# A gated mix of attention and FFN for one token: w_down's load moves from SyncE's queue to ScalarE's

## The chip, the cores and the metric

The kernel runs on one core of a Trainium2 chip. The metric is the device time of one execution in microseconds, the median of several runs. A core has TensorE (PE in the profile), VectorE (DVE), ScalarE (ACT), GpSimd (POOL) and SyncE (SP), and 16 DMA engines that bring data from the chip's main memory (HBM) into its own memory. In this kernel SyncE only issues DMAs.

## The reference

Four requests, one token each, float32. `x` is (4, 1, 512), there are 32 heads of 128, and 4096 cached positions for each head.

```python
q = (x @ wq).reshape(B, Sq, H, Dh).transpose(0, 2, 1, 3)
scores = einsum("bhqd,bhkd->bhqk", q, k_cache) * Dh ** -0.5
o = einsum("bhqk,bhkd->bhqd", softmax(scores), v_cache)
a = o.transpose(0, 2, 1, 3).reshape(B, Sq, H * Dh) @ wo        # wo: 4096 x 512
b = (gelu(x @ w_gate) * (x @ w_up)) @ w_down                   # w_down: 1792 x 512
g = sigmoid((x * gate_w).sum(-1, keepdims=True))
out = g * a + (1 - g) * b
```

The two caches are 537 MB of the 565 MB that are read.

## The kernel before, in words

The heads are taken in 8 groups of 4, and each group for each of the 4 requests: 32 blocks (`NT`). A block has 8 MB of keys and 8 MB of values, each with 64 KB on each of the 128 partitions. For a block VectorE multiplies the keys with the query (L379) and sums the products (L385), ScalarE takes the exponentials (L397), and TensorE multiplies them with the values (`pv`, L411).

All large data lie in one buffer, `big`. The keys alternate between two overlapping places at its front. The values of every block but the last lie at `VA`, and those of the last block at 0, in the place of old keys. What comes last reuses the same places: wo's first half lies in the first half of the values' place (`W0 = VA`), w_down in its second half (`D0 = VA + TW // 2`), and wo's second half in the place of the last keys (`W1 = TW`).

A small recorder, `Plan`, takes steps in the order in which the code is written. Each step names its engine and what it reads and writes in `big` or in a tile, and from that come the semaphore waits. Each engine plays its own steps in order. A DMA is a step of the engine that issues it, and the lane named with it gives the semaphore that its landing raises. `load` (L255) records every DMA as a step of SyncE, so all loads stand in one queue, in order. A step that waits holds up what stands behind it on its engine.

After the last block's scores come, in this order on SyncE's queue: the last values (lane `vl`), w_down (3584 KB), wo's first half (4096 KB in one DMA), and wo's second half in seven pieces, the last of them 128 KB each. w_down and wo's first half wait for `pv` of the last block but one, which frees the place at `VA`; wo's second half waits for the last scores.

On TensorE the tail runs as follows. `pv(NT - 1)` multiplies the last values. `turn_o(0)` transposes the attended rows of the first 16 heads (L455), `gather` collects the last group (L428), VectorE weighs it (L441), and `turn_o(1)` transposes the second 16 heads. ScalarE copies what `pv` left (`gather_a`, L419) and spreads the transposed rows (L471). Then 41 products are summed in the tile `wide` (`project_wide`, L485, which the page also shows with `hT`): 14 with the rows of w_down (`ffn_down`), 16 with the rows of wo's first half, 11 with rows of the second half. Since all of them are on TensorE, they run in the order of the code, whatever has landed. `fold` copies `wide` (L499) and adds up its four strips (L493), the last five rows of wo are multiplied in strips of their own (also L493), the result is copied (L600, L602) and stored (L603).

Of the kernel before, what the change touches and what calls it, by code (L numbers as in the profile page):

```python
# [19 lines left out]
class Plan:  # L20
# [18 lines left out]
    def add(self, engine, emit, reads=(), writes=(), lane=None, unit=1):  # L39
        lane = lane or engine  # L40
        self.units[lane] = unit
        row = self.by_lane.setdefault(lane, [])
        step = Step(lane, engine, emit, self.turn if engine in self.loops else None)
        step.at = len(row)
        need = {}
        for accesses, writing in ((reads, False), (writes, True)):
            for name, lo, hi in accesses:
                for other, a, b, wrote in self.past.get(name, ()):
                    if a < hi and lo < b and (wrote or writing):
                        if other.lane == engine and engine == "pe":  # L50
                            continue
                        if other.lane == engine and not wrote:
                            continue
                        need[other.lane] = max(need.get(other.lane, -1), other.at)
        seen = self.seen[engine]
        for l, n in sorted(need.items(), key=lambda x: -len(self.by_lane[x[0]])):
            if seen.get(l, -1) >= n:
                continue
            other = self.by_lane[l][n]
            other.asked = True  # L60
            step.waits[l] = n
            seen[l] = n
            for k, v in self.knew[other].items():
                seen[k] = max(seen.get(k, -1), v)
        step.waits = {l: n for l, n in step.waits.items()
                      if not any(self.knew[self.by_lane[m][k]].get(l, -1) >= n for m, k in step.waits.items() if m != l)}
        self.knew[step] = dict(seen)
        self.knew[step][lane] = step.at
        if row and lane == engine:
            for k, v in self.knew[row[-1]].items():  # L70
                if k != lane:
                    self.knew[step][k] = max(self.knew[step].get(k, -1), v)
        for accesses, writing in ((reads, False), (writes, True)):
            for name, lo, hi in accesses:
                old = self.past.get(name, [])
                if writing:
                    old = [x for x in old if not (lo <= x[1] and x[2] <= hi)]
                self.past[name] = old + [(step, lo, hi, writing)]
        row.append(step)
        self.steps.append(step)  # L80
        return step
# [51 lines left out]
def tile_gated_mix(tc: tile.TileContext, x, kc, vc, wq, wo, w_gate, w_up, w_down, gate_w, out):  # L133
    nc = tc.nc
    P = 128
    B, H, S, D = kc.shape
    DM = x.shape[2]
# [7 lines left out]
    NT = B * NG  # L145
    TW = R * D
# [4 lines left out]
    FC = F // P  # L151
# [62 lines left out]
    Q0, F0, F1, W0, D0 = VA, VA, VA + KC * F, VA, VA + TW // 2  # L214
# [4 lines left out]
    def place(a, n):  # L219
        return big[:, a:a + n]  # L220

    def z(a, n):
        return ("big", a, a + n)
# [15 lines left out]
    add = plan.add  # L239
# [14 lines left out]
    def load(dst, src, writes, lane):  # L254
        return add("sp", lambda: nc.sync.dma_start(dst, src), (), writes, lane=lane, unit=16)  # L255
# [10 lines left out]
    def VAT(i):  # L266
        return VA if i < NT - 1 else 0
# [3 lines left out]
             [z((F0, F1)[s], KC * F)], f"f{s}")  # L271

    def load_d():
        load(place(D0, FC * DM), w_down.rearrange("(p i) n -> p (i n)", i=FC), [z(D0, FC * DM)], "k")

    def load_w(w):
        src = wo[w * HW * D:(w + 1) * HW * D].rearrange("(p e) n -> p (e n)", e=E)
# [156 lines left out]
    def weigh(g):  # L434
        dve(lambda: V.reciprocal(ri, sm[:B * HT, D:]), t("sm"), t("ri"))
        s = sm[:B * HT, :D].rearrange("q (k e) -> q e k", e=E)
        if g < NG - 1:
            dve(lambda: V.tensor_scalar(ON[:, bass.ds(row(g), 1)], s[:, None], ri, None, op0=OP.mult), t("sm", "ri"),
                [("on", g * D, g * D + D)])
        else:  # L440
            dve(lambda: V.tensor_scalar(OX[:, :, GW - 1], s[:, :, None].to_broadcast([B * HT, E, HT, D // E]), ri, None,  # L441
                                        op0=OP.mult), t("sm", "ri"), [z(OXA, OXN)])
# [9 lines left out]
    def turn_o(w):  # L452
        def emit():
            for e in range(E):
                last = T.transpose(oT[:, e], OX[:, e].rearrange("q g h k -> q (g h k)"), ident[:B * HT, :B * HT])  # L455
            return last

        pe(emit, [z(OXA, OXN)] + t("ident"), t("oT"))
# [7 lines left out]
    def spread(w):  # L466
        n = (E, WIDE)[w]
        a, m = ES + w * E * 32, E - n
        dst = place(a, n * 32).rearrange("p (e k) -> p e k", k=8)
        src = T1[w][:, :n * B, None].to_broadcast([P, n * B, 8])  # L470
        act(lambda: A.activation(dst, src, AF.Copy), t(f"t1{w}"), [z(a, n * 32)])  # L471
        if m:
            a += n * 32
            dst2 = place(a, m * 32).rearrange("p (e k b) -> p e k b", k=8, b=B)
            src2 = T1[w].rearrange("p (e b) -> p e b", b=B)[:, n:, None, :].to_broadcast([P, m, 8, B])
            act(lambda: A.activation(dst2, src2, AF.Copy), t(f"t1{w}"), [z(a, m * 32)])
# [5 lines left out]
    def project_wide(s, w, reads):  # L482
        n = next(wide_rest)
        c = n % 4
        pe(lambda: T.matmul(wide[32 * c:32 * c + 32, :], s, w, start=n < 4, stop=n >= NW - 4), reads, t("wide"))  # L485
# [41 lines left out]
    def ffn_down(f0, f1):  # L527
        for f in range(f0, f1):
            a = D0 + f * DM
            project_wide(hT[:, f, :], place(a, DM), [("hT", f * 32, f * 32 + 32), z(a, DM)])  # L530
# [5 lines left out]
    for i in range(NT):  # L536
# [29 lines left out]
        if i > 0 and b == 0:  # L566
            weigh(g - 1)
    plan.turn = None
    load_d()
    load_w(0)  # L570
    load_w(1)
# [6 lines left out]
    gather(NG - 1)  # L578
    expand(1)
    weigh(NG - 1)  # L580
    ffn_down(0, 2)
    turn_o(1)
    turned(1)
    spread(1)
    ffn_down(2, FC)
    for e in range(E):
        project_wide(*attended(0, e))
    for e in range(WIDE):
# [56 lines left out]
```

## Time and profile before

| What | Value |
| --- | --- |
| median of 3 runs | 1309.47 us (1309.22 to 1309.71) |
| span of the profiled execution | 1308.2 us |
| mean granted TensorE clock | 0.637 |
| VectorE busy | 1155.2 us, 88% |
| TensorE busy | 355.4 us, 27% |
| ScalarE busy | 87.4 us, 7% |
| read from HBM | 564.67 MB, 432 GB/s over the span |

The span runs from the first to the last instruction of one profiled execution. No time is recorded for that execution beside its span; the median of the runs is 1.3 us more. All times in the views count from the span's start. In a view of instructions a row has the start, the duration, the engine, the line and operation, the tile written and the tiles read, the count, and in brackets how long the engine had been idle before and what ended that. "SPq" is SyncE issuing DMAs; "PEld" is TensorE loading weights, which overlaps its products. Matmuls are pipelined, and their ends are modelled.

### The profile page before, as it was taken

The numbers are of one execution on the slowest core, as the hardware profiler recorded it, in microseconds if no ns is written. First come the engines' busy times: TensorE is split into PE (matmuls) and PEld (weight loads), VectorE is DVE, ScalarE is ACT, GpSimd is POOL, SyncE is SP. The second block draws the span as 40 slices with busy tenths as digits, with TensorE's granted clock in tenths as the row PEclk, the third lists the DMA queues.
The fourth block names the chain that finished last, engine by engine and source line by source line (L and its number), as shares of the span: only waits on it lengthen the run. The fifth ranks groups of instructions, "written<-read, shape, count | busy, mean of one in ns | idle before, by whom it ended". The sixth has DMA issues, their size and how long they took to land.

```text
span 1308.2 us, 6148 instructions
## 1 busy us (share of the span) xinstructions
PE 355.4 (27%) x2504; PEld 100.7 (8%) x2504; DVE 1155.2 (88%) x299; ACT 87.4 (7%) x291; POOL 0.7 (0%) x6
## 2 busy tenths in 40 slices
PE   2402233212332211322321223331133222122327
PEld 0100001000010000100000000100001000010003
DVE  1899999999899998989989898998989899898991
ACT  0000000000000000000000000000000000000001
POOL 0000000000000000000000000000000000000000
PEclk9656666556676656666655666655566665666668
DMA  9999999999999999999999999999999999999998
GB/s 417 419 445 421 445 419 445 429 437 439 431 439 427 439 427 443 423 445 429 437 437 431 439 429 439 427 441 425 443 425 443 435 433 439 429 439 427 439 428 369
DMA packets 10977, 564.81 MB, mean 432 GB/s; under 512 B 1228, under 2 KB 1484, under 8 KB 1880
## 3 DMA queue, kind: packets, MB, share of 16 engines
q1 hardware_dynamic: 10968, 564.69, 99.7%
q8 instruction: 6, 0.10, 0.0%
q14 instruction: 3, 0.02, 0.0%
HBM read 564.67 MB, written 0.01 MB: 432 GB/s over the span
## 4 chain that ended last, share of the span: by engine, by line
DMA 72%; DVE 26%; PE 1%; issue 1%; SPq 0%; ACT 0%; DVEq 0%; POOLq 0%
DMA big<-in_A_k_cache 66%; DVE sc L385 13%; DVE big L379 12%; DMA big<-in_A_wo 2%; DMA big<-in_B_w_up 2%; DMA big<-in_A_x 2%; PE po L325 1%; PE q L506 0%; PE acc L493 0%; SPq L255 0%; PE wide L485 0%; DVE hT L525 0%; DVE m L390 0%; DVE xT L312 0%; DVE big L523 0%
## 5 line engine op out<-in xcount | busy, mean ns | idle before, releaser
L379 DVE TENSOR_TENSOR big<-big,qb 128x4096 f32<-128x4096 f32 x64 | 555.9, 8687 | 87.8 <-DMA big<-in_A_k_cache 87.8
L385 DVE TENSOR_REDUCE sc<-big 128x32 f32<-128x4096 f32 x64 | 555.9, 8686 | 2.3
L411 PE MATMUL po<-big,PM 128*32 128x512 f32 x2048 | 296.0, 743 | 899.9 <-DMA big<-in_A_v_cache 899.9
L411 PEld LDWEIGHTS po<-big,PM 128*32 128x32 f32 x2048 | 72.8, 133 | 1116.9 <-DMA big<-in_A_v_cache 824.7
L397 ACT ACTIVATE PM<-sc,nb 32x128 f32<-32x128 f32 x128 | 67.2, 525 | 478.0 <-DVE nb L392 431.3
L419 ACT ACTIVATE o<-po 128x512 f32<-128x512 f32 x16 | 9.6, 597 | 448.5 <-PE po L411 448.5
L397 ACT ACTIVATION_READ_ACCUMULATOR PM<-sc,nb 32x1 f32 x128 | 26.1, 204 | 0.0
L369 ACT ACTIVATE qb<-q 128x512 f32<-128x512 f32 x8 | 4.8, 597 | 246.9 <-PE q L367 246.9
L428 PE MATMUL sm<-o,sel 128*16 128x128 f32 x128 | 15.4, 273 | 5.1 <-ACT o L419 5.1
L312 DVE COPY xT<-sg 128x128 f32<-128x128 f32 x4 | 0.9, 282 | 17.9 <-PE sg L307 17.9
L506 PE MATMUL q<-big,xT 128*32 128x448 f32 x64 | 10.9, 853 | 15.4 <-DMA big<-in_B_w_gate 11.3
L461 DVE TENSOR_TENSOR tm<-oT,gmask 128x256 f32<-128x256 f32 x2 | 0.8, 425 | 13.8 <-PE oT L455 13.8
L428 PEld LDWEIGHTS sm<-o,sel 128*16 128x16 f32 x128 | 11.7, 97 | 12.8 <-ACT o L419 11.4
L602 DVE COPY res<-acc 4x128 f32<-4x128 f32 x1 | 0.3, 278 | 11.9 <-PE acc L493 11.9
L367 PE MATMUL q<-QM,hc 128*128 128x512 f32 x16 | 9.5, 678 | 4.2 <-DVE hc L363 4.2
L390 DVE TENSOR_REDUCE m<-sc 128x1 f32<-128x128 f32 x32 | 9.2, 286 | 1.1
L325 PE MATMUL po<-big,xT 128*32 128x512 f32 x64 | 8.5, 693 | 1.0 <-DVE xT L312 1.0
L391 DVE STREAM_TRANSPOSE mt<-m 128x32 f32<-128x32 f32 x32 | 6.8, 211 | 1.1
L485 PE MATMUL wide<-big 128*32 128x512 f32 x54 | 6.6, 597 | 1.2 <-DMA big<-in_A_wo 1.2
L392 DVE TENSOR_REDUCE nb<-mt 128x1 f32<-128x32 f32 x32 | 6.0, 186 | 1.1
L307 PE MATMUL sg<-ident,big 4*128 4x4 f32 x4 | 0.6, 254 | 23.2 <-DMA big<-in_A_x 23.2
L342 DVE TENSOR_TENSOR big<-po,amask 128x512 f32<-128x512 f32 x2 | 1.3, 686 | 5.8 <-PE po L325 5.8
(72 smaller groups left out, 58.6 us busy)
## 6 DMA issues: line engine op xcount, KB each, us to landing
big<-in_A_wo SPq DMA_DIRECT2D x1, 4096.0 KB, 27.5
big<-in_B_w_gate SPq DMA_DIRECT2D x1, 3584.0 KB, 17.4
big<-in_B_w_up SPq DMA_DIRECT2D x1, 3584.0 KB, 26.4
big<-in_B_w_down SPq DMA_DIRECT2D x1, 3584.0 KB, 18.2
big<-in_A_wo SPq DMA_DIRECT2D x2, 1024.0 KB, 25.4
big<-in_A_wo SPq DMA_DIRECT2D x2, 768.0 KB, 29.1
big<-in_A_k_cache SPq DMA_DIRECT2D x32, 29.7
big<-in_A_v_cache SPq DMA_DIRECT2D x32, 29.3
```

The lines of the kernel that those rows point to most:

```text
L325: last = T.matmul(PO[s][32 * j:32 * j + 32].rearrange("p j d -> p (j d)"), xTf[:, c, :32], w[:, n0:n0 + HB * D], start=c == 0, stop=c == K ...
L367: pe(lambda: T.matmul(q.rearrange("p b d -> p (b d)"), HC.rearrange("p h k -> p (h k)"), QM.rearrange("p b d -> p (b d)"), start=True, sto ...
L379: dve(lambda: V.tensor_tensor(k, k, QB[:, b:b + 1, :].to_broadcast([P, r1 - r0, D]), op=OP.mult), m + t("qb"), m)
L385: dve(lambda: V.tensor_reduce(SC[i % 2][:, r0:r1], k, axis=AX.X, op=OP.add), [z(KA(i) + r0 * D, (r1 - r0) * D)], [(f"sc{i % 2}", r0, r1)])
L390: dve(lambda: V.tensor_reduce(M1[n], SC[n], axis=AX.X, op=OP.max), t(f"sc{n}"), t(f"m1{n}"))
L391: dve(lambda: V.transpose(MT, M1[n].to_broadcast([P, PH])), t(f"m1{n}"), t("mt"))
L397: last = A.activation(PM[:, PZ:].rearrange("p (c m) -> p c m", m=32)[s, :, h:RJ * HT:HT], SC[n][s, :].rearrange("p (c j) -> p c j", j=RJ), ...
L411: last = T.matmul(PO[n][32 * c:32 * c + 32].rearrange("p j d -> p (j d)"), PM[:, m0:m0 + 32], place(VAT(i) + j * N, N), start=b == 0 and j ...
L419: act(lambda: A.activation(O[n], PO[n], AF.Copy), t(f"po{n}"), t(f"o{n}"))
L428: T.matmul(sm[:B * HT, :D], selv[:, j, m0:m0 + B * HT], O[n][:, j, :], start=(n, j) == (0, 0), stop=(n, j) == (N - 1, RJ - 1))
L485: pe(lambda: T.matmul(wide[32 * c:32 * c + 32, :], s, w, start=n < 4, stop=n >= NW - 4), reads, t("wide"))
L506: last = T.matmul(q.rearrange("p b d -> p (b d)")[32 * j:32 * j + 32, :FG], xTf[:, c, :32], place((F0, F1)[s] + c * F + j * FG, FG), start ...
```

## The change

w_down's load becomes a step of ScalarE: ScalarE's own queue issues it, under a lane of its own (`d`). The step names the place of the last values as read, so ScalarE waits until they have landed and then issues. The products with w_down's rows, of which two stood ahead of `turn_o(1)` and twelve behind `spread(1)`, all stand behind `spread(1)`.

```diff
     def load_d():
-        load(place(D0, FC * DM), w_down.rearrange("(p i) n -> p (i n)", i=FC), [z(D0, FC * DM)], "k")
+        add("act", lambda: nc.scalar.dma_start(place(D0, FC * DM), w_down.rearrange("(p i) n -> p (i n)", i=FC)),
+            [z(VAT(NT - 1), TW)], [z(D0, FC * DM)], lane="d", unit=16)
...
     weigh(NG - 1)
-    ffn_down(0, 2)
     turn_o(1)
     turned(1)
     spread(1)
-    ffn_down(2, FC)
+    ffn_down(0, FC)
```

On SyncE, at the end of its queue, the difference of the two programs is one row; the names are the source of each DMA, the shapes are partitions by elements:

```order
 L255 DMA big<-in_A_k_cache 128x16384
 L255 DMA big<-in_A_v_cache 128x16384 x2
-L255 DMA big<-in_B_w_down 128x7168
 L255 DMA big<-in_A_wo 128x8192
 L255 DMA big<-in_A_wo 128x2048 x2
```

wo's first half now stands right behind the last two blocks' values.

On ScalarE the changed program has this, from the last block's exponentials (`PM`) to the spread rows; its lines are one higher than before, and the brackets name the lane that a step waits for:

```order
L398 ACTIVATE PM,RS<-sc,nb 32x32x4 [waits lane_pe,lane_dve]
L398 ACTIVATE PM,RS<-sc,nb 32x32x4 x3
L274 DMA big<-in_B_w_down 128x7168 [waits lane_vl]
L420 ACTIVATE o<-po 128x512 [waits lane_pe]
L472 ACTIVATE big<-t 128x512 [waits lane_dve]
```

The DMA is new there, ahead of the copy of what `pv` left; the other rows are those of before.

On TensorE, the tail of the program before, from the last blocks' products with the values to the last wide product:

```order
L411 MATMUL po<-big,PM 32x512 x128
L455 MATMUL oT<-ident,big 128x16 x16
L428 MATMUL sm<-o,sel 16x128 x8
L430 MATMUL sm<-ones,RS 16x1
L485 MATMUL wide<-big,hT 32x512 x2
L455 MATMUL oT<-ident,big 128x16 x16
L485 MATMUL wide<-big,hT 32x512 x12
L485 MATMUL wide<-big 32x512 x27
```

And the same stretch now:

```order
L412 MATMUL po<-big,PM 32x512 x128
L456 MATMUL oT<-ident,big 128x16 x16
L429 MATMUL sm<-o,sel 16x128 x8
L431 MATMUL sm<-ones,RS 16x1
L456 MATMUL oT<-ident,big 128x16 x16
L486 MATMUL wide<-big,hT 32x512 x14
L486 MATMUL wide<-big 32x512 x27
```

All 14 products with w_down's rows (those that read `hT`) stand in one run behind the second transposes, and wo's 27 wide products follow them as before.

## The prediction

> **What bounds the kernel now.** I read the page first: shares of the span, DMA queues, the chain that ended last, DMA issues.
>
> ```profile
> span 1308.2 us, 6148 instructions
> q1 hardware_dynamic: 10968, 564.69, 99.7%
> HBM read 564.67 MB, written 0.01 MB: 432 GB/s over the span
> DMA 72%; DVE 26%; PE 1%; issue 1%; SPq 0%; ACT 0%; DVEq 0%; POOLq 0%
> big<-in_A_wo SPq DMA_DIRECT2D x1, 4096.0 KB, 27.5
> big<-in_B_w_down SPq DMA_DIRECT2D x1, 3584.0 KB, 18.2
> ```
>
> One queue, SP's, moves everything, and its packets fill the 16 DMA engines for 99.7% of the span. The kernel is a stream of 565 MB at 432 GB/s, 27 GB/s for each engine. The change leaves the bytes alone, so it acts only through the order in which the last ones arrive, and through what TensorE still has to do after them. So the second view is the timeline of the tail (columns: start, us, engine, line, operation, tiles, count, and in brackets the idle time before it and what ended that).
>
> ```profile
> 1268.09 0.33 SPq L255 DMA_DIRECT2D big<-in_B_w_down  x1
> 1268.46 10.66 SPq L255 DMA_DIRECT2D big<-in_A_wo  x8
> 1276.81 0.20 ACT L397 ACTIVATION_READ_ACCUMULATOR PM<-sc,nb 32x1 f32 x1
> 1277.99 9.95 PE L411 MATMUL po<-big,PM 128*32 128x512 f32 x64 [9.96 <-DMA big<-in_A_v_cache]
> 1288.01 0.60 ACT L419 ACTIVATE o<-po 128x512 f32<-128x512 f32 x1 [10.99 <-PE po L411]
> 1288.96 1.92 PE L428 MATMUL sm<-o,sel 128*16 128x128 f32 x16
> 1290.77 1.02 PE L485 MATMUL wide<-big,hT 128*32 128x512 f32 x3
> 1292.07 1.17 PE L455 MATMUL oT<-ident,big 16*128 16x16 f32 x16 [0.27 <-DVE big L441]
> 1293.17 2.78 PE L485 MATMUL wide<-big,hT 128*32 128x512 f32 x24
> 1296.12 4.50 PE L485 MATMUL wide<-big 128*32 128x512 f32 x40 [0.17 <-DMA big<-in_A_wo]
> 1302.76 1.06 PE L485 MATMUL wide<-big 128*32 128x512 f32 x6 [0.79 <-DMA big<-in_A_wo]
> 1303.87 0.60 ACT L499 ACTIVATE big<-wide 128x512 f32<-128x512 f32 x1 [8.96 <-PE wide L485]
> 1305.93 0.14 PEld L493 LDWEIGHTS po<-big 128*32 128x32 f32 x4 [0.17 <-DMA big<-in_A_wo]
> 1306.77 0.29 SPq L603 DMA_DIRECT2D out<-res  x1
> ```
>
> The last values land at 1278.0, where TensorE stops waiting for them. w_down lands at 1268.09 + 18.2 = 1286.3, wo's first half at 1268.46 + 27.5 = 1296.0, and the last bytes of wo about 1305.9. TensorE has nothing to catch up: w_down's rows are multiplied before wo's first half is there, so at 1296.12 and at 1302.76 it is TensorE that waits for data. The wide products end at 1302.76 + 1.06 = 1303.82, and 2.95 us later (the copy, the fold, the last five rows) the result is issued; only 0.17 us of that is a wait for wo. The tail is tight: whatever delays the wide products delays the end.
>
> **The change part by part.** *SP's queue.* It loses one issue (0.33 us). wo's first half takes w_down's place behind the last values, released by the same event (the product before the last), so the engines have no gap. wo's second half still waits for the last scores. Cost 0.
>
> *ScalarE's queue.* The new wait stands behind the last exponentials, which end at 1276.81 + 0.20 = 1277.0, and ahead of the copy of the last values' product, which ran at 1288.01 because TensorE let it. So ScalarE waits 1 us for the landing at 1278.0, issues, and has 10 us to spare. Cost 0 on the engine; without that cover every us of waiting would delay the copy by as much.
>
> *When w_down lands.* No row shows two large streams at once, so I bound it. The transfer starts at 1278.0 plus the time from an issue to its first bytes; the result's DMA needs 1308.2 - 1306.77 = 1.4 us for issue, transfer and landing together, so I take 1.0: 1279.0. Earliest: ScalarE's queue is served alone, 3.67 MB at 432 GB/s = 8.5 us, 1287.5. Latest: it is served after all of wo, about 1305.9. Between: SP has 8.4 MB of wo to move from 1277.5, so it stays busy, and equal shares give w_down 216 GB/s: 17.0 us, 1296.0, and 1296.3 with some tenths for the landing. I take the equal share, since the only foreign packets in this trace (instruction fetches, below) are let in among SP's packets and neither push them all aside nor wait for the end. wo's last bytes stay at 1305.9, since the sum of bytes is the same.
>
> *TensorE.* The two products that stood ahead of the second set of transposes saved nothing there: the transposes waited 0.27 us for VectorE anyway. Now they, the other 12, and the 27 wide products of wo, 41 in all, stand behind w_down's landing. The price of one is read off the weight loads, four for two products (each product is two records, so x40 is 20):
>
> ```profile
> 1278.82 0.22 PEld L411 LDWEIGHTS po<-big,PM 128*32 128x32 f32 x4 [0.63 <-issue]
> 1279.67 0.23 PEld L411 LDWEIGHTS po<-big,PM 128*32 128x32 f32 x4 [0.63 <-issue]
> ...
> 1297.40 0.16 PEld L485 LDWEIGHTS wide<-big 128*32 128x32 f32 x4 [0.27 <-issue]
> 1297.83 0.16 PEld L485 LDWEIGHTS wide<-big 128*32 128x32 f32 x4 [0.27 <-issue]
> ```
>
> 0.43 us for two at full clock, 0.215 each; 0.85 us, 0.425 each, at half. At full clock: 41 x 0.215 = 8.8, and 4.50 - 20 x 0.215 = 0.2 until the last is out. 1296.3 + 8.8 + 0.2 = 1305.3 instead of 1303.82 is 1.5 late; the 0.17 us wait at the end goes, since wo is there by then: **+1.3 us**. wo's wide rows are there by 1302.7, before their turn.
>
> *The clock.* TensorE now has nothing to do from 1292.07 + 1.17 = 1293.2 to 1296.3, 3.1 us, and little before. Windows of the trace (start:end and length, busy time of the engines, granted clock, DMA share, GB/s):
>
> ```profile
> 1190.00:1195.10 5.10, 0.04 (x4) 0.00 (x0) 5.10 (x1) 0.00 (x0) 0.00 (x0) 1.00 0.95 411
> 1195.10:1197.00 1.90, 0.00 (x0) 0.00 (x0) 1.83 (x3) 0.00 (x0) 0.00 (x0) 0.50 1.11 483
> 1258.60:1263.40 4.80, 4.77 (x24) 1.36 (x28) 4.77 (x2) 0.00 (x0) 0.00 (x0) 0.50 1.01 437
> 1263.40:1268.00 4.60, 4.60 (x44) 1.22 (x36) 4.60 (x1) 0.00 (x0) 0.00 (x0) 1.00 1.05 456
> 1268.00:1270.20 2.20, 0.03 (x4) 0.00 (x0) 2.20 (x1) 0.00 (x0) 0.00 (x0) 1.00 1.07 454
> 1270.20:1278.00 7.80, 0.01 (x2) 0.04 (x3) 6.08 (x8) 2.11 (x8) 0.00 (x0) 0.50 0.90 391
> 1278.00:1283.80 5.80, 5.80 (x28) 1.53 (x32) 0.00 (x0) 0.00 (x0) 0.00 (x0) 0.50 1.02 440
> ```
>
> The clock fell to half 2.2 us after the product that ended at 1268.0, and 5.1 us after the one that ended at 1190.0; once work began again it stayed at half for 4.8 us (from 1258.6) and 5.8 us (from 1278.0). Work at half clock loses half its time: 2.4 to 2.9 us, or nothing if the clock holds. An idle of 3.1 us is past the first of these falls by 0.9 and short of the second by 2.0; if the small transposes weigh little, the pause counts from the end of the gathering products (1288.96 + 1.92 = 1290.9), 5.4 us, and is past both. I take a fall, and the shorter recovery: **+2.4 us**. The Trainium skill, page "TensorE: Matmul & The Clock Gate", section "HAM oscillation — how this bites in real kernels", puts the limit at idle gaps of about 3.4 us. By that alone 3.1 us would be short enough and the sum would stay at +1.3; the 2.2 us row shows a fall earlier than that.
>
> Sum: +1.3 + 2.4 = **+3.7 us**. The span 1308.2 becomes 1311.9; the median of the runs before lies 1.3 above the span, so 1309.47 + 3.7 = **1313.2**.
>
> **The rivals.** *Equal shares, but the clock holds:* +1.3, **1310.8**. For it: the fall after 5.1 us. Against: the fall after 2.2.
>
> *Changing queues costs time.* The one place where another queue gets packets in the middle of the stream (3 us, 16 engines, so 48 us of engine time):
>
> ```profile
> q1 hardware_dynamic: 19, 1.25, 96.7%
> q8 instruction: 1, 0.02, 2.0%
> ```
>
> One 16 KB instruction packet held its engine for 2.0% of 48 = 0.96 us, where 27 GB/s makes 0.61: 0.35 more. w_down has 128 partition rows, 8 for each engine; 8 x 0.35 = 2.8 us on w_down's landing (1299.1) and on the end of the stream. With the half clock: +3.7 + 2.8 = +6.5, **1316.0**; without, 1313.6. Against: that packet went to an instruction buffer, not to big.
>
> *w_down last*, at 1305.9: the 41 products start there, 9.6 later than forecast, +13.3, **1322.8**. Nothing in the trace speaks for a preference for SP.
>
> *Served ahead, or at SP's pace in one piece:* w_down by about 1287.5, wo's first half by 1296.0 as before: **1309.5**, no change.
>
> *Faster.* Two queues keep the engines fuller. From 1277.5 to 1305.6 the 12.06 MB of w_down and wo's two halves ran at 429 GB/s; at the 454 of the window after 1268.0 they need 26.6 us and end 1.5 us earlier, at the 483 of the window after 1195.1 25.0 us, 3.1 earlier: **1306.4 to 1308.0**. It decides only if w_down also lands by about 1293, or TensorE's 9 us still set the end; over 0.2% it needs more than 473 GB/s for 28 us, where the span holds 432. The Trainium skill, "DMA: Bandwidth & Descriptors", section "Rules for kernel authors", says that spreading DMAs over issuing engines does not help bandwidth; the 99.7% agrees.
>
> **How the numbers follow.** Forecast 0.45; clock holds 0.15; queue changes 0.22; w_down last 0.05; served ahead 0.08; fuller engines 0.05. About 0.2% (2.6 us) is what a measurement of this kernel can tell from no change. Slower by more: forecast, queue changes and w_down last, 0.72. Within: clock holds, served ahead and 0.02 of the fuller engines, 0.25. Faster: 0.03. The range takes in forecast, clock held and queue changes (0.82): from 1310.8 less 0.8, if the first bytes come at once and the landing costs nothing, 1310.0, to 1316.0 and 0.5 for the longer recovery, 1316.5.
>
> **What would show it.** In the profile after: w_down on a second queue, issued by ScalarE at 1278.0, landing about 18 us later; TensorE idle from 1293.2 to 1296.3; granted clock 0.5 for some us after it; the wide products in one run without a wait for wo; their end near 1307.6; the last bytes of wo unmoved. A landing before 1290 or after 1299, a stream that ends elsewhere than 1305.9, or a clock that holds would each prove a step wrong.

## The result, and the profile after

The changed kernel takes 1315.05 us (median of 5 runs, 1314.29 to 1315.45) where the kernel before takes 1309.46: a ratio of 1.0043, 95% interval 1.003 to 1.0055. It is slower by 5.6 us, more than the 2.6 us that the prediction took as the least a measurement can tell; the forecast was 3.7 slower, with a range that reached to 1316.5. The profiled execution took 1315.45 us, 0.4 above the median.

The page after, its span, queues and the issues of the two loads (KB each, us from issue to landing):

```profile
span 1314.1 us, 6148 instructions
q1 hardware_dynamic: 10824, 561.02, 98.6%
q10 hardware_dynamic: 144, 3.67, 0.6%
big<-in_A_wo SPq DMA_DIRECT2D x1, 4096.0 KB, 25.6
big<-in_B_w_down ACTq DMA_DIRECT2D x1, 3584.0 KB, 19.3
```

q10 is ScalarE's queue: the change does what it says. The bytes are the same, and the span is 5.9 us longer. The timeline of the tail ("ACTq" is ScalarE issuing a DMA):

```profile
1278.15 0.38 ACTq L274 DMA_DIRECT2D big<-in_B_w_down  x1
1278.27 9.07 PE L412 MATMUL po<-big,PM 128*32 128x512 f32 x64 [10.87 <-DMA big<-in_A_v_cache]
1288.36 1.92 PE L429 MATMUL sm<-o,sel 128*16 128x128 f32 x16
1291.47 1.16 PE L456 MATMUL oT<-ident,big 16*128 16x16 f32 x16 [1.16 <-DVE big L442]
1297.52 5.81 PE L486 MATMUL wide<-big,hT 128*32 128x512 f32 x26 [4.89 <-DMA big<-in_B_w_down]
1303.17 6.59 PE L486 MATMUL wide<-big 128*32 128x512 f32 x52
1309.80 0.60 ACT L500 ACTIVATE big<-wide 128x512 f32<-128x512 f32 x1 [15.50 <-PE wide L486]
1312.67 0.29 SPq L603 DMA_DIRECT2D out<-res  x1
```

Up to the second transposes nothing is late: they start at 1291.47, 0.6 us sooner than before, since the last values' products took 9.07 us in place of 9.95. Then TensorE waits 4.89 us for w_down, which lands at 1278.15 + 19.3 = 1297.45, not at 1286.3. The wide products follow in one run without a wait for wo and end at 1303.17 + 6.59 = 1309.76, 5.9 later than before; from there to the store it takes 2.9 us, as before. All of the loss lies between the second transposes and the end of the wide products. The windows (start:end and length, busy us of PE, PEld, DVE, ACT and POOL, then granted clock, DMA share and GB/s):

```profile
1287.30:1292.60 5.30, 4.14 (x54) 3.75 (x50) 2.81 (x7) 1.23 (x2) 0.00 (x0) 1.00 0.93 403
1292.60:1297.50 4.90, 0.03 (x1) 0.00 (x0) 0.85 (x2) 0.72 (x2) 0.00 (x0) 0.50 0.99 419
1297.50:1302.80 5.30, 5.28 (x28) 1.35 (x32) 0.00 (x0) 0.00 (x0) 0.00 (x0) 0.50 1.00 421
1302.80:1309.80 7.00, 6.96 (x62) 1.70 (x54) 0.00 (x0) 0.00 (x0) 0.00 (x0) 1.00 0.30 116
```

The clock fell at 1292.6, just as the transposes ended, and the first 5.3 us of the 41 products ran at half clock. The DMA engines stayed full past 1302.8. In the trace the last bytes of wo end at 1305.81, where they ended at 1305.56 before, and in both 28.1 us after the last bytes of the values: the stream is not slower, only its order has changed.

### The profile page after: what moved, and what is told of

It reads as the page before. It is cut to its first block, busy times and chain, and to the rows that moved or that the text cites. A ratio compares the mean times of both kernels' runs of the same rounds, so it can differ in the third digit from the quotient of the medians.

```text
span 1314.1 us, 6148 instructions
## 1 busy us (share of the span) xinstructions
PE 355.7 (27%) x2504; PEld 100.9 (8%) x2504; DVE 1155.2 (88%) x299; ACT 87.4 (7%) x291; POOL 0.7 (0%) x6
## 3 DMA queue, kind: packets, MB, share of 16 engines
q10 hardware_dynamic: 144, 3.67, 0.6%
## 4 chain that ended last, share of the span: by engine, by line
DMA 73%; DVE 24%; PE 2%; issue 1%; ACT 0%; SPq 0%; DVEq 0%; POOLq 0%
DMA big<-in_A_k_cache 66%; DVE sc L386 12%; DVE big L380 11%; DMA big<-in_A_v_cache 2%; DMA big<-in_B_w_up 2%; DMA big<-in_A_x 2%; DMA big<-in_B_w_down 1%; PE wide L486 1%; PE po L326 1%; PE q L507 0%; PE acc L494 0%; DVE hT L526 0%; DVE xT L313 0%; SPq L255 0%; DVE big L524 0%
## 5 line engine op out<-in xcount | busy, mean ns | idle before, releaser
L486 PE MATMUL wide<-big,hT 128*32 128x512 f32 x28 | 6.2, 1001 | 4.9 <-DMA big<-in_B_w_down 4.9
## 6 DMA issues: line engine op xcount, KB each, us to landing
big<-in_B_w_down ACTq DMA_DIRECT2D x1, 3584.0 KB, 19.3
```

## The experiments

The theory: the time is w_down's landing, plus 41 products behind it, part of them at half clock because TensorE paused. The rivals: the order on TensorE costs by itself; the second queue costs by itself; the products are slow for another reason than the clock. Where a diff does not say otherwise, it is against the changed kernel. One execution of each kernel was profiled, and the rows show that one; where its time is more than 0.7 us from the median of the runs, the text says so.

### The change's two parts, one at a time

`order_only` has the order of the products alone, `queue_only` the load alone.

```diff
 order_only, against the kernel before
-    ffn_down(0, 2)
     turn_o(1)
...
-    ffn_down(2, FC)
+    ffn_down(0, FC)
 queue_only, against the changed kernel
+    ffn_down(0, 2)
     turn_o(1)
...
-    ffn_down(0, FC)
+    ffn_down(2, FC)
```

> The kernel before with the change's order on TensorE alone: w_down stays on SyncE's queue ahead of wo's first half, all 14 of its products stand behind the second transposes. If the loss hangs on when w_down lands, nothing changes, since w_down has landed at 1286.3 and the transposes waited for VectorE anyway: 1309.5, within 0.5. If the order itself costs (the rival), about 0.4 us for the two products that move behind the transposes, 1309.9, up to the whole 5.6 us, 1315.

> The changed load alone: w_down on ScalarE's queue, with two of its products ahead of the second transposes, as before. If TensorE waits for the landing of w_down near 1297.4, it now waits there with the second transposes (1.16 us) still to come: the changed kernel plus 1.2 us, 1316.2, perhaps 0.3 less where the half clock ends sooner relative to the work. If the order on TensorE were the cause (the rival), this would give back the loss: about 1310.

Measured: `order_only` 1309.82 us, ratio to before 1.0002 (0.9993 to 1.0011); `queue_only` 1316.92 us, 1.0059 (1.0045 to 1.0073). The order alone is free; the load carries the whole loss, and the old order would have made it dearer. In the timeline of `order_only` the transposes still wait for VectorE, and the 14 products fit in behind them, ahead of wo's first half:

```profile
1291.54 1.16 PE L455 MATMUL oT<-ident,big 16*128 16x16 f32 x16 [1.16 <-DVE big L441]
1292.63 3.63 PE L485 MATMUL wide<-big,hT 128*32 128x512 f32 x28
1297.01 4.50 PE L485 MATMUL wide<-big 128*32 128x512 f32 x40 [0.76 <-DMA big<-in_A_wo]
```

In that of `queue_only` the first two products wait for w_down, and the transposes with them, at half clock:

```profile
1297.06 1.92 PE L486 MATMUL wide<-big,hT 128*32 128x512 f32 x4 [6.20 <-DMA big<-in_B_w_down]
1298.91 1.88 PE L456 MATMUL oT<-ident,big 16*128 16x16 f32 x16
1300.73 4.43 PE L486 MATMUL wide<-big,hT 128*32 128x512 f32 x24
```

From w_down's landing to the end of the products (1304.98 + 6.18 = 1311.16) it took 14.1 us against 12.2, so the price was 1.9 and not 1.2: the transposes took 1.88 us where they take 1.16 at full clock, and the half clock lasted until 1304.1, 7.0 us from the landing in place of 5.3.

### The half clock, by itself

`kept_busy` gives TensorE work in the pause.

```diff
+    def keep_busy(n):
+        def emit():
+            for j in range(n):
+                c = j % 4
+                last = T.matmul(q...[32 * c:32 * c + 32], HC...[:, :32], QM..., start=True, stop=True)
+            return last
+        pe(emit, t("hc", "QM"), t("q"))
...
+    keep_busy(6)
     turn_o(1)
+    keep_busy(14)
```

> The changed kernel with 20 more products of the wide products' shape on TensorE, whose result nobody reads: 6 ahead of the second transposes and 14 behind them, 1.3 and 3.0 us at full clock, inside the pause before w_down lands. If the half clock costs 2.65 us (half of the 5.3 us that it lasted after the landing), the clock stays at 1.0, the 41 products take 8.8 us from 1297.5 and the time falls by 2.7 to 3.2 us to 1312.0. If the half clock is no cause (the rival: TensorE slowed by the transfers that go on beside it), it stays at 1315. If the clock falls even so, the added products run at half clock to about 1299 and the time rises by up to 2.

Measured: 1312.62 us, 1.0024 (1.0015 to 1.0033), 2.4 us less than the changed kernel. Its windows and its wide products, which begin at 1297.21:

```profile
1289.00:1297.20 8.20, 8.20 (x78) 4.12 (x78) 3.66 (x9) 1.35 (x3) 0.00 (x0) 1.00 0.95 405
1297.20:1307.00 9.80, 9.74 (x84) 4.39 (x82) 0.00 (x0) 0.02 (x1) 0.00 (x0) 1.00 0.79 324
...
1297.21 2.87 PE L486 MATMUL wide<-big,hT 128*32 128x512 f32 x24
1300.67 6.27 PE L486 MATMUL wide<-big 128*32 128x512 f32 x50
```

The clock stays at 1.0, w_down lands 0.3 us sooner than in the changed kernel's profile, and the 41 products take 1306.94 - 1297.21 = 9.7 us against 12.2. So it was the clock that slowed the products, and not the transfers beside them: 2.4 us of the 5.6 are the half clock. The 3.1 that are left against the kernel before go with the late landing.

### Other work in the pause

`wo_first` multiplies wo's first half ahead of w_down's rows.

```diff
-    ffn_down(0, FC)
     for e in range(E):
         project_wide(*attended(0, e))
+    ffn_down(0, FC)
```

> The changed kernel with the 16 products of wo's first half ahead of w_down's 14. wo's first half landed at 1293.0, so the products fill the pause: 16 from 1293.1, the first 4 to 5 us of them perhaps at half clock, until 1297.5 to 1299; then 25 more at 0.215, 5.4 us, until 1303.1 to 1304.6, where wo's rows land about 1303.0. Against 1303.8 before: 1309.5 to 1310.5. If the second queue costs time by itself (the rival, a slower stream or a later landing of wo), it stays above 1312.

Measured: 1309.77 us, 1.0011 (0.9993 to 1.003), with both queues as in the changed kernel. Eight of the 11 runs lie between 1309.2 and 1310.0, where the kernel before lies; the others took 1310.8, 1311.53 and 1323.12. In the median the loss is gone. The profiled execution is the one of 1311.53:

```profile
1293.11 6.55 PE L486 MATMUL wide<-big 128*32 128x512 f32 x32 [0.69 <-DMA big<-in_A_wo]
1299.47 3.19 PE L486 MATMUL wide<-big,hT 128*32 128x512 f32 x26
1302.50 3.15 PE L486 MATMUL wide<-big 128*32 128x512 f32 x20
```

The 16 products run mostly at half clock (6.55 us), and mostly in time in which TensorE had nothing to do. In this execution that time did not cover all of it: the wide products end at 1305.65, 1.8 us later than before, and its time is 1.8 above the median. What the half clock cost in the other runs was not profiled. The second queue itself costs nothing that shows here, though the interval reaches to 0.3%; `short_rows`, below, bounds it at 0.11%.

### One queue, the same late landing

`one_queue` puts both loads on SyncE's queue, w_down behind wo's first half, with TensorE's order of the changed kernel.

```diff
-        add("act", lambda: nc.scalar.dma_start(...), [z(VAT(NT - 1), TW)], [z(D0, FC * DM)], lane="d", unit=16)
+        load(place(D0, FC * DM), w_down.rearrange("(p i) n -> p (i n)", i=FC), [z(D0, FC * DM)], "k")
...
-    load_d()
     load_w(0)
+    load_d()
```

> Both loads on SyncE's queue, wo's first half first and w_down behind it; TensorE's order is that of the changed kernel. wo's first half then lands near 1288 and w_down at 1278.2 + (4.19 + 3.67) MB / 432 = 1296.4, 1.0 earlier than in the changed kernel. If what counts is the moment at which w_down lands, whatever queue brings it, the loss stays: 1314, between 1313 and 1315. If the second queue is what costs (the rival), it goes: 1309.5 to 1311.

Measured: 1313.35 us, 1.0031 (1.002 to 1.0042).

```profile
1267.28 0.42 SPq L255 DMA_DIRECT2D big<-in_B_w_down  x1
1295.72 4.74 PE L485 MATMUL wide<-big,hT 128*32 128x512 f32 x26 [3.65 <-DMA big<-in_B_w_down]
1300.30 6.59 PE L485 MATMUL wide<-big 128*32 128x512 f32 x52
```

With one queue alone the loss is there, 3.9 us of it. The profiled execution is the fastest of the seven (1312.57, 2.9 us below the profiled one of the changed kernel). Of these 2.9 us, 1.8 are w_down's sooner landing, and 1.1 are that the 41 products took 11.2 us in place of 12.2, because the half clock ended 3.1 us after the landing (at 1298.9) in place of 5.3. What counts is the landing, and the clock at that moment, not the queue.

### Who gets the DMA engines

Three kernels change the sizes of packets or the time of the issue. `short_rows` loads wo's first half in four DMAs, `halves` w_down in two, `no_wait` issues w_down without waiting for the last values.

```diff
 short_rows
-    WO_END = ((0, E), (0, 4, 8, 11, 14, 15, E))
+    WO_END = ((0, 4, 8, 12, E), (0, 4, 8, 11, 14, 15, E))
-            lane = (("q",), ("f0", "f1", "g", "v", "x", "w"))[w][n]
+            lane = (("q", "wa", "wb", "wc"), ("f0", "f1", "g", "v", "x", "w"))[w][n]
 halves
-        add("act", lambda: nc.scalar.dma_start(place(D0, FC * DM), ...), ..., lane="d", unit=16)
+        for n in range(2):
+            a, m = n * FC // 2 * DM, FC // 2 * DM
+            add("act", lambda a=a, m=m: nc.scalar.dma_start(place(D0 + a, m), ...[:, a:a + m]),
+                [z(VAT(NT - 1), TW)], [z(D0 + a, m)], lane=("d", "d2")[n], unit=16)
 no_wait
-            [z(VAT(NT - 1), TW)], [z(D0, FC * DM)], lane="d", unit=16)
+            (), [z(D0, FC * DM)], lane="d", unit=16)
```

> The changed kernel with wo's first half in four DMAs of 1 MB, so that SyncE's packets are 8 KB in place of 32 KB while w_down's stay at 28 KB. If the DMA engines take a packet of each queue in turn, w_down gets more than three quarters of the rate: the last of its packets ends near 1291 and it lands near 1291.5, wo's first half near 1296.5, and TensorE has no pause: about as before, 1309.5 to 1310.5. If the queues share by bytes, or w_down's start late after its issue is a fixed time (the rival), w_down lands near 1296 or later as it did and the time stays at 1314 to 1315.

> The changed kernel with w_down in two DMAs of 7 rows for each partition, so that its packets are 14 KB beside SyncE's 32 KB and 8 KB. By turns of packets w_down loses: its first half lands near 1292.7, its second near 1299.5, 2 us later than the whole did. The first 7 products then fill part of the pause from 1293; 34 follow from 1299.5, 7.3 us at full clock, and end near 1307.0 (1308 with some of them at half): 1312.5 to 1314. By shares of bytes (the rival) the second half lands near 1297.4 as the whole did and the end comes at 1310.5 to 1311.5.

> The changed kernel without the wait for the last values: ScalarE issues w_down right behind the last exponentials, at 1277.2, 0.95 earlier. By turns of packets the extra us is mostly given to packets beside wo's long rows and the landing moves by 0.3 to 1.0: 1314.0 to 1314.7. If the last values, whose packets are still under way at 1277.2, are held up by it (the rival), the products with them start later than 1278.2 and the time does not fall or rises.

Measured: `short_rows` 1309.84 us, 1.0002 (0.9993 to 1.0011); `halves` 1315.11, 1.0044 (1.003 to 1.0058); `no_wait` 1314.04, 1.0031 (1.0019 to 1.0043).

The queues in `short_rows`, from w_down's first packets to its last (packets, MB, share of the 16 engines), and where TensorE meets w_down:

```profile
q10 hardware_dynamic: 144, 3.67, 76.6%
q1 hardware_dynamic: 159, 1.15, 24.5%
...
1292.96 4.60 PE L486 MATMUL wide<-big,hT 128*32 128x512 f32 x26 [0.46 <-DMA big<-in_B_w_down]
```

144 packets against 159, but 3.67 MB against 1.15: near enough, the engines take a packet of each queue in turn, and the longer row wins. By shares of bytes the two would be equal. w_down lands 4.6 us sooner than in the changed kernel, the pause shrinks to 0.46 us, and the loss is gone. The clock fell here too, at 1292.4, and the first 2.9 us of the products ran at half clock; they end at 1304.1 all the same, only 0.3 us later than in the kernel before, in which TensorE waited 0.17 and 0.79 us for wo's wide rows.

`halves` goes the other way. Its 14 KB packets lose ground, and the second half comes at 1299.4, as expected:

```profile
1292.59 3.41 PE L488 MATMUL wide<-big,hT 128*32 128x512 f32 x14 [0.34 <-DMA big<-in_B_w_down]
1299.40 2.78 PE L488 MATMUL wide<-big,hT 128*32 128x512 f32 x11 [3.40 <-DMA big<-in_B_w_down]
...
1295.60:1299.00 3.40, 0.40 (x3) 0.00 (x0) 0.00 (x0) 0.00 (x0) 0.00 (x0) 0.99 0.99 414
1299.10:1302.40 3.30, 3.00 (x16) 0.80 (x20) 0.00 (x0) 0.00 (x0) 0.00 (x0) 0.50 1.01 421
```

The time missed the expected 1312.5 to 1314 by 1.1: the clock, back at full at 1295.6, fell again 3.4 us later, just ahead of the second landing, and the second half's products began 3.1 us of half clock. The expectation had counted 1 us for that (1308 for the end of the products); they end at 1301.98 + 6.84 = 1308.8.

`no_wait` issued sooner than expected, at 1275.61: ScalarE issued the DMA while its exponentials, which stand ahead of it in the program, ran on to 1277.2. It gained 2.5 us on the issue but 0.5 us on the landing (1275.61 + 21.3 = 1296.9), and 1.0 us in the median time:

```profile
big<-in_B_w_down ACTq DMA_DIRECT2D x1, 3584.0 KB, 21.3
1275.61 0.38 ACTq L274 DMA_DIRECT2D big<-in_B_w_down  x1
1278.15 8.54 PE L412 MATMUL po<-big,PM 128*32 128x512 f32 x64 [9.65 <-DMA big<-in_A_v_cache]
```

The products with the last values were not held up (1278.15). The runs scatter, though, from 1312.68 to 1314.79 against 1314.29 to 1315.45, and the profiled execution is the slowest of them. So the wait that the change adds costs something between a few tenths and 2 us; most of the 5.6 us does not come from it.

## Why the prediction was right, point by point

**Mechanism.** Right in each link but the rule of sharing (below): the issue at 1278.15 (forecast 1278.0), TensorE idle behind the second transposes, half clock behind that, no wait for wo, and the end of the wide products as what sets the end. The steps costed at nothing cost nothing: the order on TensorE (`order_only`), the wait ahead of ScalarE's own work (its copy still ran when TensorE let it, at 1287.40), and the end of the stream (1305.81 for the forecast's 1305.9).

**Sizes.** The sum was 2 us short, and these terms make that up.

*The landing*, 1297.5 for 1296.3, +1.2. The equal share of bytes was the wrong rule, and the start 1 us after the issue was wrong too, in opposite directions. In the changed kernel no packet of q10 shows in the first window below, 3.6 us from the issue; in the second it has more than half:

```profile
q1 hardware_dynamic: 48, 1.57, 101.1%
...
q10 hardware_dynamic: 85, 2.44, 57.6%
q1 hardware_dynamic: 73, 1.84, 43.6%
```

The windows are 1278.2 to 1281.8 and 1281.8 to 1291.6. A later start (-) and a larger share (+) nearly cancelled: w_down's last row ended at 1296.5 where the forecast had 1296.0. That it came so near was in part luck. The other 0.7 us is the time from there to TensorE's start, 1.0 us where the forecast had 0.3.

*The recovery of the clock*, 5.3 us for 4.8. The price by `kept_busy` is 2.4 us in the medians and 12.2 - 9.7 = 2.5 in the products, for 2.4 in the sum: at most +0.1. The Trainium skill, page "TensorE: Matmul & The Clock Gate", section "HAM oscillation — how this bites in real kernels", puts the limit at idle gaps of about 3.4 us. The real pause, 4.9 us, was past that, so this run does not decide against it; `short_rows` does, where the clock fell though TensorE's pause was 0.46 us behind the transposes, and 2.8 us (1290.2 to 1292.96) if the transposes count as nothing.

Here too the size was in part luck. In every trace the granted clock changes at whole steps of 3.41 us: in the changed kernel at 1282.3, 1292.6 and 1302.8, three steps apart, in `halves` at 1292.2, 1295.6, 1299.1 and 1302.5, one step apart. How long the half clock lasts behind a landing hangs on where in a step the landing falls: 2.9 us in `short_rows`, 3.1 in `one_queue`, 4.7 in `no_wait`, 5.3 here, 5.9 in `wo_first`.

*The products*, 9.7 us at full clock (`kept_busy`) for 9.0, +0.7. The spacing of the weight loads, 0.43 us for two products, was read rightly, but 41 is no multiple of four. The products go in turn to the four strips of `wide` (`c = n % 4` in `project_wide`), and the four run side by side: 40 take 8.6 us, and the last, alone in its strip, another 1.0. In the rows, the last product's weight loads stand one by one where four stood together before:

```profile
1304.96 0.22 PEld L486 LDWEIGHTS wide<-big 128*32 128x32 f32 x4 [0.21 <-issue]
1305.49 0.11 PEld L486 LDWEIGHTS wide<-big 128*32 128x32 f32 x1 [0.31 <-issue]
1305.92 0.11 PEld L486 LDWEIGHTS wide<-big 128*32 128x32 f32 x1 [0.32 <-issue]
```

*The end.* The 0.17 us that the forecast took off did not go: 2.91 us from the end of the products to the store, for 2.95 before and 2.78 forecast, +0.1.

Together +2.1 or 2.2, against a span 5.9 longer where 3.7 was forecast.

**Rivals.** The clock did not hold. Changing queues cost nothing that shows: from the last bytes of the values to the last of wo the stream takes 28.1 us with one queue and 28.1 to 28.3 with two, and `short_rows` and the median of `wo_first`, both with two queues, are as fast as before. So the 0.35 us of the instruction packet does not carry over to large loads. "Served ahead" is what `short_rows` came near to: its w_down landed at 1293.0, not by 1287.5, and its time was 1309.84 for the 1309.5 given there. Two queues did not fill the engines more: the rate with both was 437 GB/s in the second window above, and 437 in the first, with one.

## What to carry to other kernels

When a stream of loads is the bound, the order in which data land is the resource: moving a load to a second queue added no rate here, it shared the rate, and delayed the load that was needed first. The two queues shared by packets in turn, so the length of a row decided which got the bytes. A pause on TensorE ahead of the last burst is paid twice, once as waiting and once as half clock; work that is ready (here wo's products) belongs in it, and no version here beat the kernel before, whose order left only short pauses there (0.27, 0.17 and 0.79 us).

## What the runs showed of the hardware that was not expected

The first packets of ScalarE's queue came 3.4 to 3.7 us after their issue in all seven kernels that used it, beside the busy stream and whatever the size of SyncE's packets. In `short_rows`, where those were mostly 8 KB, the window from 1278.1 to 1281.4 again has none of q10:

```profile
q1 hardware_dynamic: 195, 1.41, 101.1%
```

So it is not a matter of a few long packets standing ahead; what it is stays open. The store of the result, on idle engines, took about 1.4 us from issue to the end of the span.

Not all work on TensorE keeps the clock up alike. Two of the clock's steps of 3.41 us, the first in the changed kernel and the second in `order_only`, have the same busy time:

```profile
1289.17:1292.58 3.41, 2.25 (x29) 2.00 (x26) 2.14 (x6) 0.63 (x1) 0.00 (x0) 1.00 0.90 388
1288.67:1292.08 3.41, 2.25 (x27) 1.99 (x24) 2.67 (x7) 0.63 (x1) 0.00 (x0) 1.00 1.02 442
```

At the end of the first the clock fell, at the end of the second it did not. The first holds 1.1 us of the gathering products and 1.1 of the small transposes, the second 1.7 and 0.5. So the transposes weigh less than the gathering products; how the weight is taken is not shown.
